# TensorE's program for seven heads as one loop body, with its waits relayed by GpSimd as tokens

## The chip, the cores and the metric

The kernel runs on one core of one Trainium2 chip. The time is device microseconds of one execution; it is about 1.3 us longer than the span of the profile page, which runs from the first to the last instruction. "Same" below means within 2%.

In the profiles PE is TensorE's matmuls and PEld its weight loads, DVE is VectorE, ACT ScalarE, POOL GpSimd, and SPq SyncE where it waits or issues; q1 and q8 are DMA queues. A semaphore is the counter that the kernel's `then_inc` raises, for an instruction or a load, and that its `wait_ge` waits for.

## The reference, cut to what matters

One token is decoded. A is attention over a cache of 65,536 keys for 8 key/value heads of width 256, with two queries per head; B is a small gated MLP; a sigmoid mixes them.

```python
q = (x @ wq).reshape(B, Sq, 16, 256)
scores = einsum("bhqd,bhkd->bhqk", q, repeat(k_cache, 2)) * 256 ** -0.5
o = einsum("bhqk,bhkd->bhqd", softmax(scores), repeat(v_cache, 2))
a = o.reshape(B, Sq, 16 * 256) @ wo
b = einsum("bsf,fd->bsd", relu(x @ W_gate) * (x @ W_up), W_down)
return g * a + (1 - g) * b            # g = sigmoid(sum(x * gate_w))
```

K and V are 2 x 8 x 65,536 x 256 bfloat16 values, 537 MB; with the weights, 549 MB have to be read once. Everything else is small beside that.

## The kernel before

The work is cut into 32 K loads and 32 V loads of 8 MB (64 KB for each of 128 partitions), which go through a ring of three SBUF slots in a fixed order. Each head has four of each. A K load is transposed in place by VectorE (eight instructions), then multiplied with the queries in two halves (QK). After the fourth K of a head comes the softmax chain, and four V loads are multiplied with the probabilities (PV). V loads run three K loads behind.

Operations are listed with a key (a planned time) and the operations that they depend on. Each engine's list is sorted by key, and the waits are made as semaphore counts:

```python
    def emit(self, e, prog, eng):
        seen = {}
        for o in prog:
            need = {}
            for d in o.deps:
                k = ("d", d.dma) if d.dma is not None else ("e", d.eng)
                need[k] = max(need.get(k, 0), d.count)
            for k, v in need.items():
                if seen.get(k, 0) < v:
                    seen[k] = v
                    eng.wait_ge(self.dsem[k[1]] if k[0] == "d" else self.esem[k[1]], v)
            ins = o.fn(eng)
            # cut: then_inc on the DMA's or on the engine's semaphore
```

The ring takes its slots in turn, and a load waits until the load that held its slot has been used:

```python
                slot[kind, i], freed[kind, i] = r, held.get(r, [])
                held[r] = [(kind, i)]
                r = (r + 1) % NRING                      # NRING = 3
```

A half of a QK product is 32 matmuls, a PV product 64. Each is a weight load and a matmul, so TensorE's program has 9,200 such instructions, all straight-line:

```python
        def f_qk(n, b, sl):
            # cut
                for c in range(4):
                    for r_ in range(2):
                        x0 = 8 + ((h * 4 + c) * 2 + r_) * 16 - 8 * b
                        for w in range(4):
                            u0 = b * 64 + w * 16
                            ins = e.matmul(bank[32 * w:32 * w + 16, :], xm[:, x0:x0 + 16],
                                           ktv[sl][:, u0:u0 + 16, c, :, r_], # cut
```

The result banks `OP`, the probabilities `ptp` and the small softmax tile `hs` exist twice, for even and odd heads.

## Time and profile before

| | before |
|---|---|
| median time | 1284.55 us (4 runs, 1283.1 to 1285.37) |
| data queue, share of the 16 DMA engines' span | 99.4% |
| TensorE, VectorE, ScalarE busy | 33%, 49%, 5% |
| instruction packets of 16 KB | 36 |

From the page of the kernel before: the busy shares, the DMA engines in 40 slices, the queue table (packets, MB, share of 16 engines), and two groups (busy us, mean ns, then the idle time ahead of them and what ended it).

```profile
span 1282.0 us, 9908 instructions
...
PE 428.3 (33%) x4600; PEld 162.3 (13%) x4600; DVE 633.6 (49%) x421; ACT 61.5 (5%) x116; POOL 4.1 (0%) x21
...
DMA  9999999999999999999999999999999999999998
...
q1 hardware_dynamic: 12930, 549.03, 99.4%
q8 instruction: 36, 0.59, 0.2%
...
DVE 34%; DMA 32%; another core or an unknown queue 16%; PE 15%; SPq 1%; ACT 1%; issue 1%
...
L335 DVE STREAM_TRANSPOSE ring<-ring 128x2048 uint32<-128x2048 uint32 x256 | 565.4, 2275 | 410.3 <-DMA ring<-in_A_k_cache_dram 410.3
L347 PE MATMUL ST<-ring,xm 128*16 128x512 bf16 x2048 | 224.9, 614 | 754.4 <-DVE ring L335 754.4
```

The data queue fills the DMA engines, and VectorE waits for K loads. Queue q8 brings 36 packets of 0.59 MB in all. These are TensorE's own instructions: 9,200 in 36 packets are some 256 to a packet.

What SyncE, which issues the loads, waits for (us in total, times, longest). L517 issues V, L452 issues K.

```profile
SPq L517 <- PE ST L347: 949.5, 30, 35.8
SPq L452 <- PE O L378: 159.2, 27, 13.1
```

A V load takes the slot of a K (its QK frees it), a K load the slot of a V (its PV frees it).

Part of the timeline of before (start, us; the bracket is the idle time before it):

```profile
569.83 17.66 DVE L335 STREAM_TRANSPOSE ring<-ring 128x2048 uint32<-128x2048 uint32 x8 [11.71 <-DMA ring<-in_A_k_cache_dram]
578.77 3.30 PE L347 MATMUL ST<-ring,xm 128*16 128x512 bf16 x32 [20.85 <-DVE ring L335]
587.54 3.59 PE L347 MATMUL ST<-ring,xm 128*16 128x512 bf16 x32 [5.47 <-DVE ring L335]
...
598.24 5.49 PE L378 MATMUL O<-ring,ptp 128*4 128x512 bf16 x64 [0.50 <-ACT ptp L494]
603.78 0.33 SPq L452 DMA_DIRECT2D ring<-in_A_k_cache_dram  x1
...
629.51 3.63 PE L378 MATMUL O<-ring,ptp 128*4 128x512 bf16 x64
629.74 0.33 SPq L517 DMA_DIRECT2D ring<-in_A_v_cache_dram  x1
633.20 0.33 SPq L452 DMA_DIRECT2D ring<-in_A_k_cache_dram  x1
647.99 17.66 DVE L335 STREAM_TRANSPOSE ring<-ring 128x2048 uint32<-128x2048 uint32 x8 [17.55 <-DMA ring<-in_A_k_cache_dram]
```

The V load issued at 629.74 is needed when the K load in flight ends, just before 647.99. TensorE idles 20 us ahead of the first QK half of a head's last K.

The page has no view of single DMA packets, but the trace holds them, with start and duration (their clock starts about 11 us ahead of the page's; the prediction's "88 to 1235 us" is in that clock). One engine around an instruction packet, in the kernel before:

```
start us   ns    bytes  queue
487.063   2420   65536  q1
489.479   1098   16384  q8      instructions
490.563   2886   65536  q1      2420 is usual
493.445   2427   65536  q1
```

The packet and the delay behind it cost this engine 1.55 us. Of the 36, 34 can be paired with the packet behind them in this way, and the median is 1.57 us.

### The profile page before, as it was taken

The page shows a single profiled execution, that of the slowest core. Times are in us where ns is not written, and L with a number is a line of the kernel's source. Part 1 is how long each engine was busy: PE and PEld are TensorE (multiplying, and loading weights), DVE is VectorE, ACT ScalarE, POOL GpSimd, SP SyncE. Part 2 cuts the span into 40 slices and gives each one's busy share as a digit, 9 for nine tenths or more (in the row PEclk, how much of TensorE's full clock was granted, in tenths as well). Part 3 has the DMA queues.
Part 4 walks back from the last instruction along what each step waited for, and adds up shares of the span by engine and source line. Part 5 has one row for each costly group of instructions (what it writes and reads, how often), then busy time and mean ns, then how long its engine had stood idle before and what let it go on. Part 6 is the DMA issues. An engine that isn't in the chain of part 4 may idle for free.

```text
span 1282.0 us, 9908 instructions
## 1 busy us (share of the span) xinstructions
PE 428.3 (33%) x4600; PEld 162.3 (13%) x4600; DVE 633.6 (49%) x421; ACT 61.5 (5%) x116; POOL 4.1 (0%) x21
## 2 busy tenths in 40 slices
PE   3623332334123431224331243321333324233245
PEld 2401110111001110001110111100111101011011
DVE  2598633465433655434555444555434555335600
ACT  0000000000000000000000000000000000000000
POOL 1000000000000000000000000000000000000000
PEclk8656666656666665667655666655666655666566
DMA  9999999999999999999999999999999999999998
GB/s 396 431 426 436 436 431 434 434 430 432 434 436 430 428 436 433 432 432 430 438 430 436 432 434 430 432 436 434 431 428 436 436 432 428 436 432 434 429 416 332
DMA packets 12975, 549.67 MB, mean 429 GB/s; under 512 B 1283, under 2 KB 3590, under 8 KB 3974
## 3 DMA queue, kind: packets, MB, share of 16 engines
q1 hardware_dynamic: 12930, 549.03, 99.4%
q8 instruction: 36, 0.59, 0.2%
q14 instruction: 5, 0.04, 0.0%
q10 hardware_dynamic: 4, 0.00, 0.0%
HBM read 549.03 MB, written 0.00 MB: 428 GB/s over the span
## 4 chain that ended last, share of the span: by engine, by line
DVE 34%; DMA 32%; another core or an unknown queue 16%; PE 15%; SPq 1%; ACT 1%; issue 1%
DVE ring L335 30%; DMA ring<-in_A_k_cache_dram 27%; PE ST L347 7%; PE O L378 6%; DMA ring<-in_B_W_up_dram 3%; DMA ring<-in_A_wo_dram 2%; DVE P_sb L480 1%; SPq L521 1%; DVE nmb L458 1%; PE PT L485 1%; PE M_ps L429 1%; PE M_ps L432 0%; ACT ptp L494 0%; DVE o_sb L389 0%
## 5 line engine op out<-in xcount | busy, mean ns | idle before, releaser
L335 DVE STREAM_TRANSPOSE ring<-ring 128x2048 uint32<-128x2048 uint32 x256 | 565.4, 2275 | 410.3 <-DMA ring<-in_A_k_cache_dram 410.3
L347 PE MATMUL ST<-ring,xm 128*16 128x512 bf16 x2048 | 224.9, 614 | 754.4 <-DVE ring L335 754.4
L347 PEld LDWEIGHTS ST<-ring,xm 128*16 128x16 bf16 x2048 | 61.6, 121 | 903.2 <-DVE ring L335 794.6
L378 PE MATMUL O<-ring,ptp 128*4 128x512 bf16 x2048 | 149.6, 455 | 33.8 <-DMA ring<-in_A_v_cache_dram 29.8
L460 ACT ACTIVATE P_sb<-ST,nmb 128x512 bf16<-128x512 f32 x32 | 45.3, 1415 | 1112.6 <-DVE nmb L458 1112.6
L458 DVE TENSOR_REDUCE nmb<-ST 128x1 f32<-128x512 f32 x32 | 22.1, 689 | 110.6 <-PE ST L347 110.6
L378 PEld LDWEIGHTS O<-ring,ptp 128*4 128x4 bf16 x2048 | 54.1, 99 | 129.2 <-issue 59.2
L389 DVE CAST o_sb<-O 128x512 bf16<-128x512 f32 x8 | 5.5, 692 | 79.7 <-PE O L378 79.7
L480 DVE TENSOR_TENSOR P_sb<-P_sb,hs 128x1024 bf16<-128x1024 bf16 x16 | 18.9, 1222 | 8.7 <-ACT hs L474 8.7
L485 PE MATMUL PT<-identb,P_sb 128*128 128x128 bf16 x128 | 16.5, 310 | 15.5 <-DVE P_sb L480 14.7
L429 PE MATMUL M_ps<-xT,ring 128*128 128x1 bf16 x84 | 9.5, 205 | 16.3 <-DMA ring<-in_B_W_up_dram 16.3
L485 PEld LDWEIGHTS PT<-identb,P_sb 128*128 128x128 bf16 x128 | 12.3, 140 | 18.3 <-DVE P_sb L480 18.3
L494 ACT COPY ptp<-PT 128x256 bf16<-128x256 bf16 x32 | 10.3, 375 | 23.0 <-PE PT L485 23.0
L307 PE MATMUL M_ps<-ring,P_sb 128*128 128x256 bf16 x64 | 10.0, 335 | 3.1 <-DMA ring<-in_A_wq_dram 3.1
L429 PEld LDWEIGHTS M_ps<-xT,ring 128*128 128x128 bf16 x84 | 7.2, 152 | 16.9 <-issue 16.5
L460 ACT ACTIVATION_READ_ACCUMULATOR P_sb<-ST,nmb 128x1 f32 x32 | 8.4, 263 | 0.0
L307 PEld LDWEIGHTS M_ps<-ring,P_sb 128*128 128x128 bf16 x64 | 7.6, 119 | 5.4 <-issue 3.2
L432 PE MATMUL M_ps<-xT,ring 128*64 128x1 bf16 x56 | 7.8, 276 | 0.0
L412 DVE STREAM_TRANSPOSE ptp<-P_sb 128x128 uint32<-128x128 uint32 x1 | 0.3, 311 | 13.4 <-ACT P_sb L411 13.4
L470 PE MATMUL M_ps<-identf,hs 128*2 128x128 f32 x8 | 2.6, 321 | 10.0 <-DVE hs L468 10.0
L432 PEld LDWEIGHTS M_ps<-xT,ring 128*64 128x64 bf16 x56 | 5.4, 191 | 0.4
L358 PE MATMUL A_ps<-ring,attnT 128*1 128x224 bf16 x64 | 4.6, 304 | 1.4 <-DMA ring<-in_A_wo_dram 1.3
(72 smaller groups left out, 60.1 us busy)
## 6 DMA issues: line engine op xcount, KB each, us to landing
ring<-in_A_v_cache_dram SPq DMA_DIRECT2D x1, 4096.0 KB, 28.7
ring<-in_A_wq_dram SPq DMA_DIRECT2D x1, 3072.0 KB, 10.4
ring<-in_A_wo_dram SPq DMA_DIRECT2D x1, 2240.0 KB, 31.4
ring<-in_A_v_cache_dram SPq DMA_DIRECT2D x1, 2048.0 KB, 23.0
ring<-in_B_W_down_dram SPq DMA_DIRECT2D x1, 1568.0 KB, 20.6
ring<-in_B_W_gate_dram SPq DMA_DIRECT2D x1, 1344.0 KB, 32.8
ring<-in_B_W_up_dram SPq DMA_DIRECT2D x1, 1344.0 KB, 35.4
ring<-in_A_v_cache_dram SPq DMA_DIRECT2D x1, 1024.0 KB, 25.0
```

The lines of the kernel that those rows point to most:

```text
L307: ins = e.matmul(QN_ps, xw3[:, k_, 31 - j:159 - j], rhs, start=(j == 0 and kt == 0), stop=(j == J - 1 and kt == R3))
L335: return lambda e: e.transpose(v, v)
L347: ins = e.matmul(bank[32 * w:32 * w + 16, :], xm[:, x0:x0 + 16], ktv[sl][:, u0:u0 + 16, c, :, r_], start=(b == 0 and c == 0 and r_ == 0), ...
L378: ins = e.matmul(OP[h % 2][32 * g:32 * g + 4, :], ptp[h % 2][:, col:col + 13:4], ring[sl][:, k * 512:(k + 1) * 512], start=(a == 0 and k < ...
L429: e.matmul(GU_ps[:, c:c + 1], wf3[which][:, kt * F + ft:(kt + 1) * F:FT], xT[:, kt:kt + 1], start=(kt == 0), stop=False, skip_group_check= ...
L432: ins = e.matmul(GU_ps[64 * half:64 * half + 64, c:c + 1], wfh[which][:, ft:F // 2:FT], xT[:, R3 + half:R3 + half + 1], start=False, stop= ...
L458: smax[n] = op("dv", tk + 22, lambda e, n=n, NM=NM, t_=t_: e.tensor_reduce(NM[:, t_:t_ + 1], ST[n % 2][:], AX.X, ALU.max, negate=True), [q ...
L460: aexp[n] = op("ac", tk + 23, lambda e, n=n, t_=t_, NM=NM, RS=RS: e.activation(P_sb[:, t_:2048:4], ST[n % 2][:], ACTF.Exp, bias=NM[:, t_:t ...
L480: rsc = op("dv", tt, lambda e, X=X, pb=pb: e.tensor_tensor(pb, pb, X[:, 12:16].unsqueeze(1).to_broadcast([128, 256, 4]), ALU.mult), [h7, a ...
L485: ins = e.transpose(PT[rd][:, s * 128:(s + 1) * 128], P_sb[:, (rd * 8 + s) * 128:(rd * 8 + s + 1) * 128], identb[:, :])
L494: ins = e.copy(dst, src)
L521: dep = dma("sp", t, "vp%d" % i, lambda e, sl=sl, n=n, lo=lo, hi=hi: e.dma_start(ring[sl][:, lo * 256:hi * 256], v_src(n)[:, lo * 256:hi * ...
```

## The change

The intent: TensorE's program for seven of the eight heads becomes one body that is run seven times. A body has fixed addresses and fixed waits, so much has to follow. The waits differ from head to head (semaphore counts grow), so GpSimd, straight-line, makes them and adds one token to a semaphore `go` per TensorE operation; TensorE waits for one token and takes it away. The slots must repeat from head to head, so the ring of three gets an order of period eight. The doubled tiles become single, and the head's queries are copied to one place (`xc`).

```diff
+    def relay(self, progs, loops):
+        for its in loops:
+            for it in its:
+                assert [o.fn.__code__ for o in it] == [o.fn.__code__ for o in its[0]]
+                for o in it:
+                    assert any(d.eng != "pe" for d in o.deps)
+                    g = _Op("gp", o.key, None, o.deps)
+                    progs["gp"].append(g)
+
+    def emit_loop(self, its, eng, go):
+        with eng.Fori(0, len(its)):
+            for o in its[0]:
+                eng.wait_ge(go, 1).then_inc(go, -1)
+                o.fn(eng).then_inc(self.esem["pe"], 1)
 ... (emit: an operation without a function is `eng.sem_inc(go, 1)`)
-        ptp = [sb("ptp%d" % i, [128, 1024], BF) for i in range(2)]
+        ptp = sb("ptp", [128, 1024], BF)
+        xc = sb("xc", [128, 136], BF)
 ... (hs, mx2 and OP single as well; their readers' dependencies move from head h - 2 to h - 1)
+        ROUND = (0, 1, 2, 0, 1, 0, 2, 1)
-                slot[kind, i], freed[kind, i] = r, held.get(r, [])
-                held[r] = [(kind, i)]
-                r = (r + 1) % NRING
+                m = r - 3
+                sl = r if m < 0 else ROUND[m % 8] if m < 8 * (H - 1) else m % 8 % 3
+                slot[kind, i], freed[kind, i] = sl, held.get(sl, [])
+                held[sl] = [(kind, i)]
+                r += 1
 ...
+                if t_ == 0:
+                    xcopy = op("ac", tk + 1, lambda e, h=h: e.copy(xc[:, 8:136], xm[:, 8 + h * 128:136 + h * 128]),
+                               [l_["xm"], qk.get((n - 1, 1)), c_xc])
 ...
+        pe = progs["pe"]
+        cut = [pe.index(qk[h * NTH + NTH - 1, 0]) for h in range(H)]
+        its = [pe[a:b] for a, b in zip(cut, cut[1:])]
+        go = es.enter_context(nc.semaphore("go"))
+        pl.relay(progs, [its])
 ...
-        pl.emit("pe", progs["pe"], nc.tensor)
+        pl.emit("pe", pe[:cut[0]], nc.tensor)
+        pl.emit_loop(its, nc.tensor, go)
+        pl.emit("pe", pe[cut[-1]:], nc.tensor)
```

More of the change, by code (lines that the diff above doesn't have):

```diff
@@ L71, in finish, with emit @@
         return progs
-    def emit(self, e, prog, eng):
-        seen = {}
+    def relay(self, progs, loops):
[11 more added lines that the diff above has]
+                o.fn(eng).then_inc(self.esem["pe"], 1)
+    def emit(self, e, prog, eng, go=None, seen=None):
+        seen = {} if seen is None else seen
         for o in prog:
@@ L83, in emit @@
                     eng.wait_ge(self.dsem[k[1]] if k[0] == "d" else self.esem[k[1]], v)
+            if o.fn is None:
+                eng.sem_inc(go, 1)
+                continue
             ins = o.fn(eng)
@@ L132, in bass_gated_mix__gqa_block_cached__glu_gated_reglu__decode_kernel @@
         P_sb = sb("P_sb", [128, 2048], BF)
-        ptp = [sb("ptp%d" % i, [128, 1024], BF) for i in range(2)]
+        ptp = sb("ptp", [128, 1024], BF)
+        scr = sb("scr", [128, 1024], BF)
+        xc = sb("xc", [128, 136], BF)
         xm = sb("xm", [128, H * 128 + 8], BF)
@@ L147, in bass_gated_mix__gqa_block_cached__glu_gated_reglu__decode_kernel @@
         selc = sb("selc", [128, 10], F32)
-        mx2 = sb("mx2", [2, 2], F32)
+        mx2 = sb("mx2", [2, 1], F32)
         nmb = [sb("nmb%d" % i, [128, NTH], F32) for i in range(2)]
         rs = [sb("rs%d" % i, [128, NTH], F32) for i in range(2)]
-        hs = [sb("hs%d" % i, [128, 20], F32) for i in range(2)]
+        X = sb("hs", [128, 20], F32)
         attnT = sb("attnT", [128, H * 4], BF)
@@ L161, in bass_gated_mix__gqa_block_cached__glu_gated_reglu__decode_kernel @@
         fin_o = P_sb[0:1, 0:D]
-        gw_row = ptp[1][0:1, 0:D]
-        xeo = ptp[1][0:1, 448:704]
-        qrep = ptp[1][:, 704:960]
-        gtmp = ptp[0][0:1, 0:2 * D].bitcast(F32)
+        gw_row = scr[0:1, 0:D]
+        xeo = scr[0:1, 448:704]
+        qrep = scr[:, 704:960]
+        gtmp = ptp[0:1, 0:2 * D].bitcast(F32)
         wq3 = ring[2][:, 0:R3 * NQ]
@@ L177, in bass_gated_mix__gqa_block_cached__glu_gated_reglu__decode_kernel @@
         PT = [ps("PT%d" % i, [128, 1024], BF) for i in range(2)]
-        OP = [ps("O%d" % i, [128, 512], F32) for i in range(2)]
+        OP = ps("O", [128, 512], F32)
         A_ps = ps("A_ps", [128, 512], F32)
@@ L244, in bass_gated_mix__gqa_block_cached__glu_gated_reglu__decode_kernel @@
         c_xm = op("dv", 0.021, lambda e: e.memset(xm[:], 0.0))
+        c_xc = op("dv", 0.022, lambda e: e.memset(xc[:, 0:8], 0.0))
         def f_mask(e):
@@ L251, in bass_gated_mix__gqa_block_cached__glu_gated_reglu__decode_kernel @@
         c_ps = []
-        for i, tt in enumerate([ST[0], ST[1], OP[0], OP[1]]):
+        for i, tt in enumerate([ST[0], ST[1], OP]):
             c_ps.append(op("dv", 0.04 + i * 0.001, lambda e, tt=tt: e.memset(tt[:], 0.0)))
@@ L337, in f_qk @@
         def f_qk(n, b, sl):
-            h = n // NTH
             bank = ST[n % 2]
@@ L343, in f @@
                     for r_ in range(2):
-                        x0 = 8 + ((h * 4 + c) * 2 + r_) * 16 - 8 * b
+                        x0 = 8 + (c * 2 + r_) * 16 - 8 * b
                         for w in range(4):
                             u0 = b * 64 + w * 16
-                            ins = e.matmul(bank[32 * w:32 * w + 16, :], xm[:, x0:x0 + 16], ktv[sl][:, u0:u0 + 16, c, :, r_],
+                            ins = e.matmul(bank[32 * w:32 * w + 16, :], xc[:, x0:x0 + 16], ktv[sl][:, u0:u0 + 16, c, :, r_],
                                            start=(b == 0 and c == 0 and r_ == 0), stop=(b == 1 and c == 3 and r_ == 1),
@@ L377, in f_pv @@
                     col = k * 16 + a
-                    ins = e.matmul(OP[h % 2][32 * g:32 * g + 4, :], ptp[h % 2][:, col:col + 13:4],
+                    ins = e.matmul(OP[32 * g:32 * g + 4, :], ptp[:, col:col + 13:4],
                                    ring[sl][:, k * 512:(k + 1) * 512],
@@ L383, in make_pv @@
             tp = max(tv, last["tev", h])
-            deps = [dep] + last["ev", h] + ([last.get(("ocp", h - 2)), c_ps[2 + h % 2]] if a == 0 else [])
+            deps = [dep] + last["ev", h] + ([last.get(("ocp", h - 1)), c_ps[2]] if a == 0 else [])
             pv[n] = op("pe", tp, f_pv, deps)
             if a == NTH - 1 and hi == U:
-                X = hs[h % 2]
                 tn = tp + (8.0 if n < NT - 1 else 1.2)
-                o1 = op("dv", tn, lambda e: e.tensor_copy(o_sb[:], OP[h % 2][:]), [pv[n], last.get(("otr", h - 1))])
+                o1 = op("dv", tn, lambda e: e.tensor_copy(o_sb[:], OP[:]), [pv[n], last.get(("otr", h - 1))])
                 def f_otr(e):
@@ L454, in bass_gated_mix__gqa_block_cached__glu_gated_reglu__decode_kernel @@
                 tr = [op("dv", tk + 2.22 * w, f_trans(sl, w), [kd]) for w in range(8)]
+                if t_ == 0:
+                    xcopy = op("ac", tk + 1, lambda e, h=h: e.copy(xc[:, 8:136], xm[:, 8 + h * 128:136 + h * 128]),
+                               [l_["xm"], qk.get((n - 1, 1)), c_xc])
                 for b in range(2):
-                    qk[n, b] = op("pe", tk + 9 * (b + 1), f_qk(n, b, sl), [tr[4 * b + 3], l_["xm"], aexp.get(n - 2), c_ps[n % 2]])
+                    qk[n, b] = op("pe", tk + 9 * (b + 1), f_qk(n, b, sl), [tr[4 * b + 3], xcopy, aexp.get(n - 2), c_ps[n % 2]])
                 NM, RS = nmb[h % 2], rs[h % 2]
@@ L464, in bass_gated_mix__gqa_block_cached__glu_gated_reglu__decode_kernel @@
                     T = tk + 9
-                    X = hs[h % 2]
                     h1 = op("dv", T + 13.5, lambda e, X=X, NM=NM: e.tensor_reduce(X[:, 0:1], NM[:], AX.X, ALU.min),
-                            [smax[n], last.get(("norm", h - 2))])
+                            [smax[n], last.get(("norm", h - 1))])
                     h2 = op("dv", T + 13.6, lambda e, X=X: e.scalar_tensor_tensor(X[:, 2:4], selc[:, 2:4], X[:, 0:1], selc[:, 4:6], ALU.mult, ALU.add),
@@ L470, in bass_gated_mix__gqa_block_cached__glu_gated_reglu__decode_kernel @@
                     h3 = mop("pe", T + 14, lambda e, X=X: e.transpose(VT_ps, X[:, 2:4], identf[:, :]), [h2, g_idf])
-                    h4 = mop("dv", T + 14.5, lambda e, h=h: e.tensor_reduce(mx2[0:2, h % 2:h % 2 + 1], VT_ps, AX.X, ALU.max), [h3])
-                    h5 = mop("pe", T + 15, lambda e, h=h: e.matmul(NMR_ps, nselT[0:2, :], mx2[0:2, h % 2:h % 2 + 1], start=True, stop=True), [h4, l_["ns"]])
+                    h4 = mop("dv", T + 14.5, lambda e, h=h: e.tensor_reduce(mx2[0:2, 0:1], VT_ps, AX.X, ALU.max), [h3])
+                    h5 = mop("pe", T + 15, lambda e, h=h: e.matmul(NMR_ps, nselT[0:2, :], mx2[0:2, 0:1], start=True, stop=True), [h4, l_["ns"]])
                     h6 = mop("ac", T + 15.3, lambda e, X=X: e.copy(X[:, 4:5], NMR_ps), [h5])
@@ L492, in f_ev @@
                                 src = PT[rd][:].rearrange("p (u w r) -> p u w r", u=8, w=4)[:, :, :, 8 * b:8 * b + 8]
-                                dst = ptp[h % 2][:, b * 512:(b + 1) * 512].rearrange("p (w u r) -> p u w r", w=4, u=16)[:, rd * 8:rd * 8 + 8, :, :]
+                                dst = ptp[:, b * 512:(b + 1) * 512].rearrange("p (w u r) -> p u w r", w=4, u=16)[:, rd * 8:rd * 8 + 8, :, :]
                                 ins = e.copy(dst, src)
                             return ins
-                        q = op("ac", tt + 1, f_ev, [p, pv.get((h - 1) * NTH - 1)])
+                        q = op("ac", tt + 1, f_ev, [p, pv.get(h * NTH - 1)])
                         last["bank", rd] = q
@@ L558, in bass_gated_mix__gqa_block_cached__glu_gated_reglu__decode_kernel @@
         nc.sync.wait_ge(pl.dsem["out"], 16)
-        pl.emit("pe", progs["pe"], nc.tensor)
         pl.emit("dv", progs["dv"], nc.vector)
-        pl.emit("gp", progs["gp"], nc.gpsimd)
+        pl.emit("gp", progs["gp"], nc.gpsimd, go)
+        pl.emit("pe", pe[:cut[0]], nc.tensor)
+        pl.emit_loop(its, nc.tensor, go)
+        pl.emit("pe", pe[cut[-1]:], nc.tensor)
     return nc
```

## The prediction

Cuts in the recorded text are marked. Item 2: its sum keeps both cases, 0 to +0.9 us and -2.4 us, and the forecast came to 1284.4 us beside 1284.55 us measured for the kernel before. Item 4 loses the price of a token, an estimate that named no measured hop, with the delays of the first PV and of QK that followed from it; its "five" are five of TensorE's 18 operations per head. Item 5, the term for tokens: with it the slack came to the 13 us that stand further down, without it to 14.

> **What bounds it now.** The DMA engines. The page's queue table gives the data queue 99.4% of 16 engines' span; the slices stand at 9 throughout. In the trace's packet records a 64 KB packet takes 2.42 us with almost no spread, and each engine starts the next as the last ends: from 88 to 1235 us I find under 0.5 us idle on any engine. 549 MB at 433 GB/s (16 x 64 KB / 2.42 us) is 1267 us; head and tail are the rest. TensorE (33%) and VectorE (49%) have slack. Only a full queue and the tail (last landing near 1276.5 us, then 5 us of work) matter.

> **What the change does.**
> 1. The data moved stays: 0 us.
> 2. Instruction pages. The queue table shows 36 packets of 16 KB for instructions. In the packet records one costs its engine 1.55 us (its own 1.1, and the data packet behind it takes 2.89 instead of 2.42); 36 x 1.55 / 16 = 3.5 us of the span. [...] The loop body has about 1090 TensorE instructions, over 4 pages. Fetched anew each time, the count stays at 36 to 45 (0 to +0.9 us); kept, about 25 pages go (-2.4 us). I hold the first likelier, 2 to 1.
> 3. The branch falls after a head's output transpose (ends 558 us in the timeline) and before the next QK (578.8 us): TensorE only waits there. A stall of some us is hidden.
> 4. Tokens: [...] five lie on a head's softmax chain (592 to 598 us)[...]. The load it releases is needed no sooner than 628. The last head, the tail, is outside the loop.
> 5. Ring order: two V loads per head now reuse the slot of the V two loads before. The V issued at 629.7 us (after a QK) will wait for the PV before it, at 633.2. The queue then still holds a K load until 647: slack shrinks from 17.5 to 14 us[...]. Other loads keep distance 3 or 4.
> 6. Single buffers (O, ptp, hs, mx2): their last readers finish (558 us) before the next head's softmax writes (592). The extra copy of the head's queries (ScalarE, under 0.5 us) runs beside 18 us of transposes.

> On the critical path: only item 2.

> **Predicted: 1284.4 us, 8 in 10 between 1281.5 and 1287.5.** Faster by over 2%: 0.01. Within 2%: 0.96. Slower by over 2%: 0.03.

> **What would show it.** The data queue stays at 99.4%, 64 KB packets at 2.42 us, VectorE's idle time still ended by K landings. Instruction packets tell item 2: 36 to 45, or about 11. SyncE's waits for PV (O) grow and those for QK (ST) shrink, yet no gap between packets opens. [...] TensorE's matmul count is unchanged.

> **What would make it wrong.** A token hop of several us, eating the 13 us of slack; a loop entry that stalls over 20 us, or a stall at each page; engines so uneven that a load ends over 10 us late on one of them, so that a shorter queue leaves others idle; a single buffer's wait that I overlooked, seen as ScalarE or TensorE released late and gaps in the queue.

## The result, and the profile after

| | before | after |
|---|---|---|
| median time (4 runs each) | 1284.55 us | 1279.85 us (1278.19 to 1280.26) |
| ratio | 1 | 0.9962, 95% interval 0.9945 to 0.9979 |
| instruction packets of 16 KB | 36 | 11 |
| data queue's share | 99.4% | 99.6% |

A ratio is the mean time of one kernel's fast runs over that of the other's in the same rounds, so it isn't quite the ratio of the medians. The change gains 4.9 us by that ratio (0.0038 x 1284.4 us). By the 2% rule it is "same", as predicted, but the time lies below the predicted range.

From the page after, the lines that answer to those of before:

```profile
span 1278.8 us, 10158 instructions
...
PE 427.7 (33%) x4600; PEld 169.4 (13%) x4600; DVE 633.1 (50%) x421; ACT 63.1 (5%) x124; POOL 4.1 (0%) x21
...
DMA  9999999999999999999999999999999999999998
...
q1 hardware_dynamic: 12930, 549.03, 99.6%
q8 instruction: 11, 0.18, 0.1%
...
DMA 2%; DVE 2%; PE 2%; another core or an unknown queue 1%; SPq 1%; ACT 0%; issue 0%
...
L360 DVE STREAM_TRANSPOSE ring<-ring 128x2048 uint32<-128x2048 uint32 x256 | 565.4, 2275 | 399.0 <-DMA ring<-in_A_k_cache_dram 399.0
L371 PE MATMUL ST<-ring,xc 128*16 128x512 bf16 x2048 | 224.9, 614 | 745.8 <-PEq L86 687.6
```

TensorE's matmul time and VectorE's work are the same to 0.2%. Of 36 instruction packets 25 are gone: the loop body isn't fetched again. The chain of waits is now nearly empty (its shares add up to some 8%, against 100% before), because it can't be followed back through a token: a QK that waits for a token is put down to TensorE's own sequencer ("PEq L86"), not to the transpose behind it. It must not be read as less waiting.

SyncE's waits (L542 issues V, L475 issues K):

```profile
SPq L542 <- PE ST L371: 518.8, 16, 34.7
SPq L542 <- PE O L402: 469.1, 14, 39.5
SPq L475 <- PE O L402: 116.8, 14, 13.7
```

The V loads that reuse a V's slot are there: 14 of them now wait for a PV. The timeline after, same stretch of work:

```profile
568.64 17.66 DVE L360 STREAM_TRANSPOSE ring<-ring 128x2048 uint32<-128x2048 uint32 x8 [11.40 <-DMA ring<-in_A_k_cache_dram]
577.75 3.33 PE L371 MATMUL ST<-ring,xc 128*16 128x512 bf16 x32 [20.71 <-PEq L86]
586.50 3.59 PE L371 MATMUL ST<-ring,xc 128*16 128x512 bf16 x32 [5.42 <-PEq L86]
...
597.90 5.19 PE L402 MATMUL O<-ring,ptp 128*4 128x512 bf16 x64 [0.54 <-PEq L86]
603.15 0.33 SPq L475 DMA_DIRECT2D ring<-in_A_k_cache_dram  x1
...
628.51 3.63 PE L402 MATMUL O<-ring,ptp 128*4 128x512 bf16 x64
632.18 0.33 SPq L542 DMA_DIRECT2D ring<-in_A_v_cache_dram  x1
...
646.06 17.66 DVE L360 STREAM_TRANSPOSE ring<-ring 128x2048 uint32<-128x2048 uint32 x8 [16.63 <-DMA ring<-in_A_k_cache_dram]
```

Half of the eight transposes take 8.83 us; QK starts 0.11 us after them before and 0.28 us after: a token costs 0.17 us. From the start of the second QK half to the first PV it was 10.70 us and is 11.40. The V load is issued at 632.18, 13.9 us before the next K's transposes begin; no gap between loads opens.

**Where the 4.9 us came from.** Each of the sixteen DMA engines ends its share of a load with a write of 4 bytes to the load's semaphore; the packet records hold sixteen per load. The last write releases what waits: in the kernel before, the transposes of 30 K loads start 0.37 to 0.55 us behind the last write of their load, and 2.8 to 7.7 us behind the first. For the 2nd and the 57th of the loads that end after 85 us in that clock, sorted, in us after the first engine of the same load:

```
before,  2nd   0.0 0.1 0.1 0.3 0.3 0.6 0.7 0.7 | 0.9 1.0 1.1 1.2 1.3 1.4 1.8 2.7
before, 57th   0.0 0.0 0.7 0.8 1.2 1.3 2.6 2.7 | 5.5 5.9 6.1 6.3 6.4 6.4 7.2 7.2
after,   2nd   0.0 0.0 0.2 0.2 0.3 0.3 0.3 0.3 | 0.4 0.4 0.8 1.0 1.2 1.3 1.8 2.8
after,  57th   0.0 0.1 0.2 0.4 0.4 0.8 1.0 1.0 | 1.4 1.8 1.9 1.9 2.2 2.2 2.9 2.9
```

The records carry no engine number, but an engine can be followed: a packet starts within some 15 ns of the end of the one before it on its engine, and each engine has eight packets of a load and then its semaphore write. Followed in this way, each of the 17 instruction packets between 600 and 1215 us in the kernel before leads to one of the last five of its load's sixteen writes; in filler_late (below) 24 of 27 lead to one of the last seven, and three can't be told. None leads to one of the first eight.

The averages hide this. The windows view (us, busy time by engine, granted clock, DMA share, GB/s) of before and of after has the same rate in the long middle:

```profile
88.00:1176.00 1088.00, 348.20 (x3775) 121.03 (x3779) 561.57 (x343) 53.86 (x101) 0.00 (x0) 0.61 1.00 433
```

```profile
88.00:1176.00 1088.00, 350.09 (x3823) 129.13 (x3823) 562.75 (x345) 56.04 (x109) 0.00 (x0) 0.62 1.00 433
```

All engines are busy in both; the fast eight only run ahead. The debt is paid at the end, where they have nothing left: from 88 us to the last data packet the sixteen engines together stand idle for 24 to 28 us in the three kernels with 36 packets, 1 to 11 us in the three with 11 or 12, and 58 us in filler_late with 54, all of it after 1240 us on the page's clock.

### The profile page after: what moved, and what is told of

Its sections match the earlier page's. It is cut to its first block, busy times and chain, and to the rows that moved or that the text cites. A ratio compares the mean times of both kernels' runs of the same rounds, so it can differ in the third digit from the quotient of the medians.

```text
span 1278.8 us, 10158 instructions
## 1 busy us (share of the span) xinstructions
PE 427.7 (33%) x4600; PEld 169.4 (13%) x4600; DVE 633.1 (50%) x421; ACT 63.1 (5%) x124; POOL 4.1 (0%) x21
## 3 DMA queue, kind: packets, MB, share of 16 engines
q1 hardware_dynamic: 12930, 549.03, 99.6%
## 5 line engine op out<-in xcount | busy, mean ns | idle before, releaser
L371 PE MATMUL ST<-ring,xc 128*16 128x512 bf16 x2048 | 224.9, 614 | 745.8 <-PEq L86 687.6
L371 PEld LDWEIGHTS ST<-ring,xc 128*16 128x16 bf16 x2048 | 66.7, 121 | 889.6 <-issue 827.2
L510 PE MATMUL PT<-identb,P_sb 128*128 128x128 bf16 x128 | 16.2, 307 | 16.7 <-PEq L86 13.9
```

The lines of the kernel that those rows point to most:

```text
L371: ins = e.matmul(bank[32 * w:32 * w + 16, :], xc[:, x0:x0 + 16], ktv[sl][:, u0:u0 + 16, c, :, r_], start=(b == 0 and c == 0 and r_ == 0), ...
L510: ins = e.transpose(PT[rd][:, s * 128:(s + 1) * 128], P_sb[:, (rd * 8 + s) * 128:(rd * 8 + s + 1) * 128], identb[:, :])
```

## The experiments

Theory A: an instruction packet costs 1.55 us on one of eight engines, so 1.55 / 8 = 0.19 us of the whole (an estimate from the records above), and nothing else in the change matters. Theory B: it costs a sixteenth, 0.10 us, as the prediction had it, and other edits give the other half. Theory C: ring order and single buffers give it all.

| run | packets of 16 KB | median us | ratio to before | 95% interval |
|---|---|---|---|---|
| straight | 36 | 1284.19 | 1.0003 | 0.9989 to 1.0017 |
| tokens_unrolled | 36 | 1284.55 | 1.0007 | 0.9993 to 1.0021 |
| loop_three | 28 | 1282.91 | 0.9992 | 0.9979 to 1.0006 |
| filler | 48 | 1294.38 | 1.0078 | 1.0064 to 1.0092 |
| after_again | 11 | 1280.37 | 0.9970 | 0.9956 to 0.9984 |
| body_padded | 12 | 1280.30 | 0.9968 | 0.9954 to 0.9981 |
| two_heads | 41 | 1284.98 | 1.0006 | 0.9993 to 1.0020 |
| filler_late | 54 | 1287.31 | 1.0025 | 1.0011 to 1.0038 |

Five rounds each; the first four beside one set of runs of before (median 1283.79 us), the last four beside another (1284.19 us).

### straight: the change without loop and tokens

```diff
-        pl.relay(progs, [its])
-        pl.emit("gp", progs["gp"], nc.gpsimd, go)
-        pl.emit("pe", pe[:cut[0]], nc.tensor)
-        pl.emit_loop(its, nc.tensor, go)
-        pl.emit("pe", pe[cut[-1]:], nc.tensor)
+        pl.emit("gp", progs["gp"], nc.gpsimd)
+        pl.emit("pe", pe, nc.tensor)
```

> The change without its loop and tokens: TensorE's program straight-line again with its own waits; ring order, single buffers and the query copy stay. Theory A (an instruction page costs 1.55 us on one of eight engines, so 0.19 us of the whole per page, and nothing else matters): about 36 pages of 16 KB again, ratio to before 1.000 within 0.001; the spread of the sixteen engines' ends of a load grows to about 7 us again. Theory B (a page costs a sixteenth, 0.10 us, and the other edits give the other half): ratio 0.998. Theory C (ring order and buffers give it all): ratio 0.996.

Measured 1.0003. The queue table's line for TensorE's instructions:

```profile
q8 instruction: 36, 0.59, 0.2%
```

Ring order, single buffers and the query copy are all in it, and nothing is gained: theory C falls, and B with it, whose 0.998 lies outside the interval too. The engines' ends spread over 7.7 us at the 57th load, as in the kernel before.

### tokens_unrolled: the tokens without the loop

```diff
-        with eng.Fori(0, len(its)):
-            for o in its[0]:
+        for it in its:
+            for o in it:
```

> The tokens stay, the loop is unrolled: seven copies of the body in TensorE's program. Theory A: 36 or 37 pages, ratio to before 1.000 within 0.001 (tokens cost nothing, being off the path, and gain nothing). Theory B or C: 0.996 to 0.998. If the tokens themselves gained something, this would be faster than the straight variant; I expect the two within 0.001 of each other.

Measured 1.0007 with 36 packets, 0.0004 from the run above and inside its interval. The tokens neither gain nor cost what can be seen here. Its interval, too, excludes what B and C expected. What is left of the change is the loop itself.

### loop_three: three heads in the loop, four straight-line

```diff
+        its = its[:3]
         pl.relay(progs, [its])
...
-        pl.emit("pe", pe[cut[-1]:], nc.tensor)
+        pl.emit("pe", pe[cut[3]:], nc.tensor)
```

> Only three of the seven heads run in the loop, four are straight-line. Two passes are saved, 2 x about 1090 instructions, 8 or 9 pages: 27 or 28 pages remain. Theory A: -1.6 us, ratio 0.9987. Theory B: -3.2 us, 0.9975. Theory C: 0.996.

```profile
q8 instruction: 28, 0.46, 0.1%
```

The count is as expected. Measured 0.9992 (-1.0 us), between the kernel before and the change. The interval holds A (0.9987) and excludes C; B's value, 0.9975, lies just outside it. The interval holds 1 as well, so that this run alone shows no gain.

### filler: a dose of packets, badly placed

```diff
+            if o in pad:                       # pad: qk[n, 0] for all 32 n
+                for _ in range(200):
+                    eng.wait_ge(self.esem["dv"], 1)
             ins = o.fn(eng)
```

> The kernel before, with 200 waits that are met already put into TensorE's program ahead of each first QK half (6400 instructions, 25 pages), where TensorE is idle over 9 us anyway. Theory A: about 61 pages, +4.8 us, ratio 1.0038, and the spread of the engines' ends near 1176 us grows from 7 to about 12 us, eight engines staying where they were. Theory B: +2.4 us, 1.0019. Theory C: 1.000.

This was +10 us, twice what A expected, but for a fault of the experiment. TensorE isn't idle over 9 us everywhere: in the trace of before it idles 7.0 and 8.8 us ahead of two of the first halves and not at all ahead of the first K's. The waits were joined in pairs when the program was built (3,200 instructions more in the profile, not 6,400; 48 packets, not 61), and the fillers ahead of the first K's QK (about 9 us) held up the MLP's last matmuls behind it, which free a ring slot. SyncE's wait for them was 36.3 us before:

```profile
SPq L455 <- PE A_ps L361: 47.8, 1, 47.8
```

The landings are 9 us late from the first load after 85 us on (the second of them at 121.2 against 112.1 us in the packet clock). What remains of the +10 us, some 1 to 2, is too coarse to tell A from B. So it was made again, see filler_late.

### after_again: the changed kernel once more

> The changed kernel itself, beside the others on one chip. 11 pages against 36. Theory A (0.19 us per page): -4.8 us, ratio 0.9963. Theory B (0.10 us per page, the rest from something else): the same here by construction, since it was made from this number.

Measured 0.9970, -3.9 us: a little less than the first 0.9962, and the two intervals overlap for the most part.

### body_padded: a longer body

Waits that are met already, 480 instructions in all, are added in four places of the body where TensorE idles, so that it has 1570 instructions instead of 1090 (6.1 packets instead of 4.3).

```diff
             for o in its[0]:
+                if o in pad:                   # the first QK halves
+                    for _ in range(240):       # joined in pairs: 120
+                        eng.wait_ge(self.esem["dv"], 1)
                 eng.wait_ge(go, 1).then_inc(go, -1)
```

> The changed kernel with 480 more instructions (waits that are met already, in 4 places where TensorE is idle) in the loop body: 1570 instead of about 1090. If a body of over 6 pages of 16 KB is kept as well, the count of pages is 13 or 14 and the ratio to before 0.9966; if it is fetched anew on every pass, 6 or 7 pages times 7, over 50 pages in all, and slower than before by 3 us or more, 1.002.

```profile
q8 instruction: 12, 0.20, 0.1%
```

Measured 0.9968 with 12 packets (13 or 14 were expected). The body runs seven times and is fetched once. That TensorE goes through 3,360 more instructions costs nothing visible; only what is fetched counts.

### two_heads: a body too long to be kept

```diff
+        its = [its[i] + its[i + 1] for i in (0, 2, 4)]
         pl.relay(progs, [its])
...
-        pl.emit("pe", pe[cut[-1]:], nc.tensor)
+        pl.emit("pe", pe[cut[6]:], nc.tensor)
```

> The body holds two heads (about 2180 instructions, 8.5 pages), run three times; the seventh head is straight-line. If a body of that length is kept: 36 less 2 x 8.5 pages, 19 or 20, ratio by theory A 0.9975. If it is not kept: about 36 to 40 pages and 1.000 to 1.001, although the program in memory is nearly halved: then it is the fetched pages that count and not the length of the program.

```profile
q8 instruction: 41, 0.67, 0.2%
```

TensorE's program in memory is nearly halved and it loops, and yet 41 packets are fetched (36 to 40 were expected for a body that isn't kept; tokens_unrolled, the same work straight-line, fetched 36) and the time is 1.0006. So the gain isn't a shorter program, nor looping as such; it is the packets that are not fetched.

### filler_late: the dose again

As filler, but 260 waits ahead of the first and 80 ahead of the second QK half, and none for the first four K loads.

```diff
+            for _ in range(pad.get(o, 0)):     # {qk[n, b]: (260, 80)[b] for n in range(4, NT) ...}
+                eng.wait_ge(self.esem["dv"], 1)
```

> The kernel before with 4760 fillers (waits that are met already) in TensorE's program, none ahead of the first four K loads: in the first filler run half the waits had been joined in pairs, and those ahead of the first K held it up by some 9 us. 18 or 19 pages more than 36. Theory A: +3.6 us, ratio 1.0028, and the spread of the engines' ends of a load near 1176 us at 10 to 11 us instead of 7.2. Theory B: +1.8 us, 1.0014. Neither: 1.000.

```profile
q8 instruction: 54, 0.88, 0.3%
```

Measured 1.0025, +3.2 us for 18 packets more: A expected +3.6, B +1.8. The interval holds both A's 1.0028 and B's 1.0014, so that the time alone doesn't decide; the landings do. At the 57th load:

```
filler_late   0.0 0.0 0.1 0.2 0.6 0.8 1.3 3.5 | 9.1 9.2 9.3 9.5 9.6 10.0 11.8 11.9
```

Eight engines stay together, the other eight are now over 9 us late. The first engine still needs 1064.3 us from the 2nd to the 57th load, the last one 1073.4. This is the plainest evidence of where the packets go.

A straight line through the eight timed runs other than the misplaced filler (each run's ratio, less 1, times 1284.1 us, against its packets less 36, forced through zero and weighted by the intervals) has a slope of 0.17 us per packet, standard error 0.02. A's 0.19 lies about one standard error off, B's 0.10 about three and a half. (Runs that share a set of runs of before share its noise, which this leaves out.) Over 25 packets that is 4.3 us, between the 4.9 and 3.9 us measured.

### Three looks: how long may the body be?

body_padded with 352, 430 and 472 waits per place instead of 240. These are single runs for the packet count. Their times are no test: if 200 waits take some 9 us, as in filler, 352 to 472 take some 16 to 21 us (an estimate), and in the trace of after TensorE idles only 12.3 to 13.7 us ahead of one first half of each head.

> One look, for the count of pages only: the loop body filled up to about 1794 TensorE instructions, 7.0 pages of 256. [...] it is kept: 13 or 14 pages. [...] it is not: 40 pages or more.

> The same with about 1950 instructions, 7.6 pages. [...] 14 pages in all if kept, over 45 if not. Its time is no test: the fillers before a first QK half take longer than TensorE is idle there.

> The same with about 2034 instructions, 7.9 pages[...]. [...] I expect it is not kept: over 45 pages.

The q8 lines of body_1794, body_1950 and body_2034, in this order:

```profile
q8 instruction: 67, 1.10, 0.3%
```

```profile
q8 instruction: 74, 1.21, 0.4%
```

```profile
q8 instruction: 74, 1.21, 0.4%
```

None is kept. I had thought 1794 and 1950 might be; both miss. In the packet records the body of 1090 instructions is fetched in the first pass only: no instruction packet comes between 244 and 1180 us of the page's clock. Here each of the six later passes brings 9 packets in body_1794 and 10 in the other two, more than the 7.0, 7.6 and 7.9 pages of the body: it is fetched whole each time. Without these 54 and 60 packets, 13 and 14 would be left, the count expected of a kept body. In these runs the limit lies between 1570 and 1794 instructions; what it counts is left open. The three took 1290.6 to 1293.9 us (before: 1283.57 us), but how much of that is packets and how much the held-up TensorE isn't shown. That a body that is too long gains nothing rests on two_heads.

## Why the prediction was right or wrong

**What bounds it: right.** DMA engines without a pause, before and after.

**Branch, tokens, ring order, single buffers (items 3 to 6): right that they are off the path.** Straight and tokens_unrolled show it for items 4 to 6 (1.0003 and 1.0007). They have no branch; in the timeline after, the QK at 577.75, the first after the branch, starts 0.28 us behind its transposes, as does the one at 616.46 inside the body, so that the branch costs nothing there. The slack of the V load was put at 13 to 14 us and is 13.9. A token hop is 0.17 us, and the first PV came 0.7 us later in its chain; the copy of the head's queries takes ScalarE 0.31 us (L479 of after). No size among these matters.

**Item 2, instruction packets: the right mechanism, two errors in it.** What failed is this step: "36 x 1.55 / 16 = 3.5 us of the span", and from it "kept, about 25 pages go (-2.4 us)". The 25 were exact, and the 1.55 us per packet hold (median 1.57). The divisor was wrong. The packets fall on eight engines, and the kernel ends with the slowest: 25 x 1.55 / 8 = 4.8 us, where -4.9 and -3.9 were measured. I had divided by all sixteen because no engine ever idled in the middle. But that says only that the fast engines had work queued; it doesn't say that they finish together. The ends of the loads, which were in the trace before, spread from 2.7 to 7.2 us and would have shown it.

The second error is the weight "I hold the first likelier, 2 to 1", that the body is fetched on each pass. No trace had shown that, and a body of over four pages is kept: 11 packets in all for seven passes. With the body kept and the wrong divisor the prediction would still have been near 1282; with the right divisor, the case held likelier would have read 1284.5 to 1286.3 and the other 1279.7.

TensorE itself was not seen to wait for a fetch: with 36 packets as with 11, no matmul within a group of QK or PV starts more than 0.43 us behind the last one until 1268 us, where the last V loads come in.

**Left open:** why a packet of 16 KB costs its engine 1.57 us when a data packet of that size takes 0.61 us in the same trace, and why eight engines.

## What to carry to other kernels

In this kernel, which fills the DMA engines (99.4%), TensorE's own instructions were traffic that cost time: look at the instruction queue's line on the page, and price each packet on the engine that carries it, not on all of them (here 0.17 us of the whole for each, not 0.10). Where work is split evenly over parallel servers without stealing, a cost that falls on some of them is shared by those alone, and the slowest sets the end; compare when each finishes, since busy shares and mean rates can't show it (here both kernels moved 433 GB/s, while at the 57th load the last engine was 7.2 us behind the first in one and 2.9 in the other). A loop pays here if its body is short enough to be kept (1570 instructions were, 1794 were not), so measure the packet count first: a body of two heads, over the limit, fetched more (41 packets) than the same work straight-line (36).
